# Two chunks of a weight product in float32r from split parts, and one activation load issued a chunk sooner

## The chip, the cores and the metric

The kernel runs on one core of one Trainium2 chip. The metric is the device time of one execution in microseconds (us). One execution was recorded by the hardware profiler; its rows carry the line of the kernel (L573 is line 573), the engine and the tiles. PE is the matrix engine, PEld its weight loads, DVE the vector engine, ACT the scalar engine, POOL the general-purpose engine, SP the engine that issues most DMAs. A row with SPq is an issue by SP's sequencer.

## The reference

Attention against a small state in both directions, then a bilinear layer with no nonlinearity but a product, the weights in float64 on their way into the chip:

```python
def _attn_ref(x, state):                  # x: 8 x 8 x 512 x 64, state: 8 x 8 x 32 x 64
    ...
    xread = np.matmul(a, state)           # a = softmax(x state^T / 8)
    ...
    sread = np.matmul(a2, x)              # a2 = softmax(state x^T / 8)
    return np.concatenate([xread, sread], axis=2).astype(np.float32)

def _moe_ref(x, w1, w2, w3, w_out):       # x: 4352 x 512 here; w1, w2: 512 x 1024
    a = x @ w1
    b = x @ w2
    h = a * b @ w3                        # w3: 1024 x 1024
    return (h @ w_out).astype(np.float32) # w_out: 1024 x 512
```

Since nothing stands between w3 and w_out, the kernel multiplies these two once, at its start (w34 = w3 w_out, 1024 x 512), and uses the result for all tokens.

## The kernel before

**Stages.** The program has a prologue of about 70 us and then eight batches. A batch multiplies the attention weights by state-times-w1 and state-times-w2 (stage 1, L321), takes the product of the two results, and multiplies it by w34 (stage 2, L335, and for batches 1 to 7 the quarters of L435 to L453). A row block of read states follows at the end. The prologue makes w34, the first attention scores and the first weights of stage 1. The change lies in the prologue alone.

**The loads and their conversion.** The weights arrive as float64 bits, 1 MB for a tile of 128 x 1024 words. `to_f32` (L103 to L137) loads such a tile into one of three `raw` buffers (L115, issued by SP) and makes float32 of it: on ACT the high words (L119, Prelu), then the low words into `ulps` (L127); after its `yield` on DVE a shift (L131) and the adding of the two (L135). The raw buffer is free again when L127 has read it. Loads 0 and 1 are done in two parts, the others in one.

**The order of the prologue.** PE, SP, ACT and DVE run in the order of the program there (`manual_schedule`, L65 and L609). `w34_k[k]`, k = 0 to 7, holds in one tile w_out's k-th 128 rows (512 columns) and four blocks of w3 for the same k (512 columns). L612 to L615 convert such a tile per step and, two steps later, multiply it: `w34_first` (L570 to L576) has four float32 products of 128 x 128 by 128 x 512 per k, each adding to one of four PSUM sums. In steps 8 and 9 two blocks of another tensor, w3t, are loaded and converted (`convert_w3`, L578). Behind the loop come, in this order:

- `load_x(0)` (L616): st and x_d of batch 0, 64 KB and 1 MB, issued by SP;
- the scores of batch 0 on PE (L148, from `scores`, L180);
- `finish(0)`, `finish(1)` and a split of the sums 2 and 3 together (L620 to L622): a cast on ACT (L98) and a subtraction on DVE (L99), which give the high and low part of w34 in float32r;
- `w34(4)` (L623): eight products by the block of w3t that step 8 converted, into the PSUM bank that `finish(0)` has read;
- the conversion of w1 and w2 and of the last two w3t blocks, the softmax of batch 0 (L187 to L233), `w34(5)`, `w34(6)`, and so on.

`split` (L95) is used all over: `hi` is a float32r copy of its source by ACT, `lo` the difference by DVE. Stage 1 has three products for each full one: hi by lo, hi by hi, lo by hi. `sw_pair` (L272) takes a pair of float32r tiles of 128 x 2 x 512 from a rotation of four.

Of the kernel before, what the change touches and what calls it, by code (L numbers as in the profile page):

```python
# [29 lines left out]
P = 128  # L30
NF = 512
NW = 1024
AHEAD = 2
LAST = 5
PARTS = {0: (640, 1024), 1: (512, 1024)}
WARM = 15
PLAIN = 1

@with_exitstack
def attn_bilinear_kernel(  # L40
# [10 lines left out]
    nc = tc.nc  # L51
# [5 lines left out]
    FT, DO = w34_k.shape[0], out.shape[2]  # L57
# [31 lines left out]
    def bank():  # L89
        return ps_o.tile([P, NF], F32, name="ps_o")  # L90

    def two_banks():
        return ps_2.tile([P, 2, NF], F32, name="ps_2")

    def split(hi, lo, src):  # L95

        return (
            nc.scalar.copy(out=hi, in_=src),  # L98
            nc.vector.tensor_tensor(out=lo, in0=src, in1=hi.bitcast(F32), op=ALU.subtract),  # L99
        )  # L100


    def to_f32(pool, src, out, ends=(NW,), loads=(), wout=None):  # L103

        raw = pool.tile([P, NW], mybir.dt.int64, name="raw", bufs=3)
        ulps = pool.tile([P, NW], I32, name="ulps", bufs=2)
        parts = [slice(*ends) for ends in zip((0, *ends), ends)]
        for start, stop in zip((0, *loads), (*loads, NW)):
            nc.sync.dma_start(out=raw[:, start:stop], in_=src[:, start:stop])  # L115
        for part in parts:
            words = raw[:, part].bitcast(I32).rearrange("p (n k) -> p k n", k=2)
            high, low = words[:, 1], words[:, 0]
            nc.scalar.activation(  # L119
                out=out[:, part], in_=high.bitcast(F32), func=AF.Prelu, scale=2.0**-112, alpha=-(2.0**32)  # L120
            )
            if len(parts) > 1:
                nc.vector.tensor_scalar(
                    out=ulps[:, part], in0=low.bitcast(U32), scalar1=2.0**-29, scalar2=None, op0=ALU.mult
                )
            else:
                nc.scalar.activation(out=ulps[:, part], in_=low.bitcast(U32), func=AF.Copy, scale=2.0**-29)  # L127
        yield
        for part in parts:
            bits = out[:, part].bitcast(I32)  # L130
            nc.vector.tensor_scalar(out=bits, in0=bits, scalar1=3, scalar2=None, op0=ALU.logical_shift_left)  # L131
            for dest, start, stop in ((wout, 0, DO), (out, DO, NW)) if wout is not None else ((out, 0, NW),):
                piece = slice(max(start, part.start), min(stop, part.stop))
                if piece.start < piece.stop:
                    nc.vector.tensor_tensor(  # L135
                        out=dest[:, piece].bitcast(I32), in0=out[:, piece].bitcast(I32), in1=ulps[:, piece], op=ALU.add
                    )  # L137
# [14 lines left out]
    def load_x(b):  # L152
        sts[b] = att.tile([P, NP, NS], F32, name="st")
        nc.sync.dma_start(out=sts[b], in_=st[b])
        x_tiles[b] = att.tile([P, NP, S], F32, name="x_d", bufs=1)
        nc.sync.dma_start(out=x_tiles[b], in_=x_d[b])
# [8 lines left out]
    def work_tile():  # L165
        return att.tile([P, KT, S], F32, name="work")
# [9 lines left out]
    def attention_steps(b):  # L176
# [3 lines left out]
        def scores():  # L180
# [15 lines left out]

            first, second = (maxima, turn) if b > PLAIN else (turn, maxima)
            with tc.issue_after(first().ins):
# [4 lines left out]
            for kt in range(KT):  # L203
# [3 lines left out]
                )  # L207
            if b > PLAIN:
                yield
# [27 lines left out]
            with tc.issue_after(last[1].ins):  # L237
                nc.vector.transpose(out=flat(blocks), in_=flat(e2))
            a2["t"] = work_tile() if b < PLAIN else att.tile([P, KT, S], F32, name="e2", bufs=1)
            tiles = lambda t: t.rearrange("p k (t m) -> p (k t) m", m=P)  # L240
# [31 lines left out]
    def sw_pair():  # L272
        return [main.tile([P, KT, NF], F32R, name=f"sw_{part}", bufs=2 * HALF) for part in ("hi", "lo")]
# [244 lines left out]
    def quarter_batch(b):  # L518
        q = {"raw": []}
        softmax = iter(())  # L520
        for ft in range(FT):
# [19 lines left out]
            elif ft == 4:  # L541
                next(softmax, None)
            if b == PLAIN and ft == 1:
                combine_weights(QF - 1)
# [4 lines left out]
    def run(steps):  # L549
        for step in steps:  # L550
            for _ in step() or ():
                pass


    with tc.tile_pool(name="pro", bufs=2) as pro:

        places = [w_sb[:, n // 2, n % 2].rearrange("p j f -> p (j f)") for n in range(2 * QT)]
        w_out = [places[(FT + k) // 2][:, k % 2 * DO:(k % 2 + 1) * DO] for k in range(FT)]

        chunks = [places[k % (FT // 2)] for k in range(FT)]  # L560
        w3s, w34_ps = {}, {}

        def finish(i):
            split(wo["hi"][:, i], wo["lo"][:, i], w34_ps[i][:, :DO])

        def convert_first(k):
            ends = PARTS.get(k, (NW,))
            return to_f32(pro, w34_k[k], chunks[k], ends, (), wout=w_out[k])

        def w34_first(k):  # L570

            for i in range(FT // 2):
                nc.tensor.matmul(  # L573
                    w34_ps[i][:, :DO], chunks[k][:, DO + i * P:DO + (i + 1) * P], w_out[k],
                    start=(k == 0), stop=(k == FT - 1),
                )  # L576

        def convert_w3(i):  # L578
            w3s[i] = pro.tile([P, NW], F32, name="w3", bufs=2)
            return to_f32(pro, w3t[i - FT // 2], w3s[i])  # L580

        def w34(i, ks=range(FT)):
            if ks[0] == 0:
                w34_ps[i] = bank()
            for k in ks:
                nc.tensor.matmul(  # L586
                    w34_ps[i][:, :DO], w3s[i][:, k * P:(k + 1) * P], w_out[k], start=(k == 0), stop=(k == FT - 1)
                )

        def convert_half(n):  # L590

            return to_f32(pro, w12[n], places[n])

        def sets(quarter):
            for i in range(2):
                sw_quarter(0, quarter, i)


        gs, acc, early = [], [], range(2)

        def early_stage2(quarter):
            if quarter == 0:
                acc.extend(bank() for _ in early)
            for ft in range(2 * quarter, 2 * quarter + 2):
                for tt in early:
                    project(acc[tt], gs, tt, ft)

        order = ctx.enter_context(ExitStack())
        order.enter_context(tc.manual_schedule(engines={mybir.EngineType.Activation, mybir.EngineType.DVE}))  # L609
        pair = two_banks()  # L610
        w34_ps.update(enumerate([bank(), bank(), pair[:, 0], pair[:, 1]]))
        for k in range(FT + AHEAD):  # L612
            run([partial(convert_first, k) if k < FT else partial(convert_w3, k - FT // 2)])
            if k >= AHEAD:
                w34_first(k - AHEAD)  # L615
        load_x(0)  # L616
        scores, reads[0], _ = attention_steps(0)
        softmax = scores()
        next(softmax)
        finish(0)  # L620
        finish(1)
        split(wo["hi"][:, 2:4], wo["lo"][:, 2:4], pair[:, :, :DO])  # L622
        w34(4)  # L623

        w1_0, w2_0, w1_1, w2_1 = map(convert_half, range(4))
        go = lambda steps: next(steps, None)
        w3_6 = convert_w3(6)
        go(w1_0), go(softmax), go(w1_0)
        finish(4)
        go(w2_0), go(w3_6), go(softmax), go(w3_6)  # L630
        w34(5)
        go(softmax)
        go(w2_0)
        finish(5)
        w3_7 = convert_w3(7)
        go(w3_7), go(w3_7), go(w1_1), go(w1_1), go(w2_1), go(w2_1)
        load_tokens(0)
        w34(6)
        sets(0)
        finish(6)  # L640
        w34(7, range(LAST))
        sets(1)
        w34(7, range(LAST, FT))
        finish(7)
        order.close()
        for quarter in range(QT):
            stage1(0, 2 * quarter, gs)
            if quarter == 1:
                run(sw_steps(0)[2:])
            if quarter:  # L650
                early_stage2(quarter - 1)
            if quarter == 1:
                side = side_steps()
            elif quarter == 2:
                run(side.pop(0))
            stage1(0, 2 * quarter + 1, gs)
            if quarter == 0:
                run([partial(convert_half, n) for n in range(4, 2 * QT)])
                load_x(1)
                with tc.issue_after(last_split[1].ins):  # L660
                    go(softmax)
        run(side.pop(0))
        early_stage2(QT - 1)
# [42 lines left out]

    for b in range(PLAIN, B):
        quarter_batch(b)
# [46 lines left out]
```

## Time and profile before

| | |
|---|---|
| median of 3 runs | 490.66 us (490.65 to 491.01) |
| the profiled execution | 490.49 us |
| its span, first to last instruction | 488.7 us |
| mean granted PE clock | 0.998 |
| HBM read, written | 38.27 MB, 8.91 MB |

The span is shorter than the time of its execution by what lies before the first and behind the last instruction. Busy times are unions of an engine's instructions. A matmul of float32 gives two records, one of float32r gives one, and the end of each is modelled, so that rates are read from start to start. In the view of 40 equal slices PE is busy in every slice, and DMA is busiest in the first six, which are the prologue.

### The profile page before, as it was taken

The page shows a single profiled execution, that of the slowest core. Times are in us where ns is not written, and L with a number is a line of the kernel's source. Part 1 is how long each engine was busy: PE and PEld are TensorE (multiplying, and loading weights), DVE is VectorE, ACT ScalarE, POOL GpSimd, SP SyncE. Part 2 cuts the span into 40 slices and gives each one's busy share as a digit, 9 for nine tenths or more (in the row PEclk, how much of TensorE's full clock was granted, in tenths as well). Part 3 has the DMA queues.
Part 4 walks back from the last instruction along what each step waited for, and adds up shares of the span by engine and source line. Part 5 has one row for each costly group of instructions (what it writes and reads, how often), then busy time and mean ns, then how long its engine had stood idle before and what let it go on. Part 6 is the DMA issues. An engine that isn't in the chain of part 4 may idle for free.

```text
span 488.7 us, 8603 instructions
## 1 busy us (share of the span) xinstructions
PE 482.1 (99%) x3390; PEld 368.9 (75%) x3390; DVE 391.0 (80%) x576; ACT 235.5 (48%) x364; POOL 0.2 (0%) x4
## 2 busy tenths in 40 slices
PE   8999999999999999999999999999999999999996
PEld 6444467767787878887888788877977797899885
DVE  5669897699899679958995899599859985678870
ACT  4767784454357144704570556055515541353640
POOL 0000000000000000000000000000000000000000
PEclk9999999999999999999999999999999999999999
DMA  8996981153114404130413041304230223001101
GB/s 343 359 368 242 369 307 27 18 206 73 37 20 165 118 15 166 48 98 4 180 37 96 4 181 41 90 5 180 44 86 6 89 44 87 5 2 43 45 1 44
DMA packets 56361, 52.49 MB, mean 107 GB/s; under 512 B 42752, under 2 KB 50944, under 8 KB 51712
## 3 DMA queue, kind: packets, MB, share of 16 engines
q1 hardware_dynamic: 47488, 43.27, 27.0%
q10 hardware_dynamic: 8832, 8.65, 5.2%
q8 instruction: 27, 0.44, 0.4%
q14 instruction: 14, 0.11, 0.1%
HBM read 38.27 MB, written 8.91 MB: 97 GB/s over the span
## 4 chain that ended last, share of the span: by engine, by line
PE 77%; DVE 7%; SPq 6%; ACT 5%; DMA 3%; issue 1%; ACTq 0%; DVEq 0%
PE ps L321 29%; PE ps_o L435 11%; PE ps L447 8%; PE ps L148 6%; SPq L172 6%; PE ps_o L440 5%; PE ps L452 4%; PE ps L693 3%; PE ps_o L573 3%; PE ps L573 3%; PE ps_o L335 2%; DMA raw<-in_w_dram 2%; PE ps L695 2%; ACT ulps L127 2%; PE ps_o L253 1%
## 5 line engine op out<-in xcount | busy, mean ns | idle before, releaser
L321 PE MATMUL ps<-at_lo,sw_hi 128*128 128x512 f32 x256 | 101.3, 396 | 0.2 <-ACT e L205 0.2
L321 PE MATMUL ps<-at_hi,sw_hi 128*128 128x512 f32 x256 | 99.7, 390 | 0.0
L321 PE MATMUL ps<-at_hi,sw_lo 128*128 128x512 f32 x256 | 99.7, 389 | 0.0
L525 ACT COPY tmp<-ps 128x512 f32<-128x512 f32 x56 | 32.8, 585 | 121.6 <-PE ps L321 121.1
L321 PEld LDWEIGHTS ps<-at_lo,sw_hi 128*128 128x128 f32 x256 | 48.1, 188 | 16.9 <-DVE g_lo L99 4.2
L321 PEld LDWEIGHTS ps<-at_hi,sw_lo 128*128 128x128 f32 x256 | 48.1, 188 | 10.3
L321 PEld LDWEIGHTS ps<-at_hi,sw_hi 128*128 128x128 f32 x256 | 48.1, 188 | 9.4 <-issue 0.2
L463 DVE TENSOR_TENSOR tmp<-tmp,ps 128x512 f32<-128x512 f32 x42 | 28.8, 687 | 17.8 <-PE ps L452 16.9
L404 DVE TENSOR_TENSOR g_x<-tmp,ps 128x512 f32<-128x512 f32 x28 | 19.0, 678 | 28.1 <-ACT tmp L525 28.1
L99 DVE TENSOR_TENSOR sw_lo<-ps,sw_hi 128x1024 fp32r<-128x1024 f32 (+1 forms) x34 | 38.2, 1145 | 1.5 <-ACT sw_hi L98 1.5
L98 ACT CAST g_hi<-raw 128x512 fp32r<-128x512 f32 x42 | 24.6, 619 | 28.1 <-DVE raw L404 20.7
L435 PEld LDWEIGHTS ps_o<-t,g_hi 128*128 128x128 f32 x224 | 27.7, 191 | 5.5 <-issue 5.0
L148 PE MATMUL ps<-w_sb,st 64*32 64x512 f32 (+1 forms) x544 | 31.4, 570 | 0.0
L98 ACT CAST sw_hi<-ps 128x1024 fp32r<-128x1024 f32 (+1 forms) x34 | 31.1, 966 | 0.6 <-PE ps L148 0.5
L98 ACT CAST g_hi<-g_x 128x512 fp32r<-128x512 f32 x42 | 25.5, 626 | 11.4 <-DVE g_x L404 6.0
L435 PE MATMUL ps_o<-t,g_hi 128*128 128x256 f32 x224 | 29.8, 286 | 0.3 <-ACT tmp L483 0.3
L99 DVE TENSOR_TENSOR g_lo<-raw,g_hi 128x512 fp32r<-128x512 f32 x42 | 27.9, 678 | 1.7 <-PE ps_o L440 1.6
L435 PE MATMUL ps_o<-wo,g_hi 128*128 128x256 f32 x224 | 29.1, 283 | 0.0
L435 PEld LDWEIGHTS ps_o<-wo,g_hi 128*128 128x128 f32 x224 | 28.3, 192 | 0.5
L586 PE MATMUL ps_o<-w_sb,w 128*128 128x512 f32 x64 | 28.5, 599 | 0.0
L99 DVE TENSOR_TENSOR g_lo<-g_x,g_hi 128x512 fp32r<-128x512 f32 x42 | 27.1, 679 | 1.8 <-PE ps_o L440 1.8
L447 PE MATMUL ps<-t,g_hi 128*128 128x512 f32 x112 | 28.0, 392 | 0.0
(103 smaller groups left out, 784.6 us busy)
## 6 DMA issues: line engine op xcount, KB each, us to landing
raw<-in_w_k_dram SPq DMA_DIRECT2D x8, 1024.0 KB, 6.7
x_d<-in_x_d_dram SPq DMA_DIRECT2D x8, 1024.0 KB, 6.8
raw<-in_w_dram SPq DMA_DIRECT2D x8, 1024.0 KB, 6.8
x_s<-in_x_s_dram SPq DMA_DIRECT2D x8, 1024.0 KB, 5.0
out_dram<-tmp ACTq DMA_DIRECT2D x56, 128.0 KB, 1.8
raw<-in_w3t_dram SPq DMA_DIRECT2D x4, 1024.0 KB, 7.4
e<-work SPq DMA_DIRECT2D x112, 32.0 KB, 2.0
sread<-turned SPq DMA_DIRECT2D x128, 4.0 KB, 1.7
```

The costliest lines, as they stand in the source:

```text
L98: nc.scalar.copy(out=hi, in_=src),
L99: nc.vector.tensor_tensor(out=lo, in0=src, in1=hi.bitcast(F32), op=ALU.subtract),
L148: nc.tensor.matmul(ps[j * NS:(j + 1) * NS, q], sts[b][rows, j], moving(rows, j), start=True, stop=True)
L172: nc.sync.dma_start(out=dest(slice(c * NS, (c + 1) * NS), j), in_=src(slice(j * NS, (j + 1) * NS), c))
L321: nc.tensor.matmul(ps[:, i], w[:, kt, c:c + P], a[:, kt], start=(k == 0), stop=(k == 3 * KT - 1))
L435: nc.tensor.matmul(ps[:, tt * HO:(tt + 1) * HO], g, w(part, k), start=(fresh and k == 0 and tt == 0 and part == "lo"), stop=False, skip_gr ...
L440: nc.tensor.matmul(ps[:, tt * HO:(tt + 1) * HO], g, w("hi", k), start=False, stop=(k == QF - 1), skip_group_check=True)
L447: nc.tensor.matmul(ps[:, tt].rearrange("p (n d) -> p n d", n=2), g, w(k), start=(k == 0), stop=False, skip_group_check=True,)
L463: sum2 = lambda out, x, y: nc.vector.tensor_tensor(out=out, in0=x, in1=y, op=ALU.add)
L525: copied = nc.scalar.copy(out=a_sb, in_=ps[:, 0])
L573: nc.tensor.matmul(w34_ps[i][:, :DO], chunks[k][:, DO + i * P:DO + (i + 1) * P], w_out[k], start=(k == 0), stop=(k == FT - 1),)
L586: nc.tensor.matmul(w34_ps[i][:, :DO], w3s[i][:, k * P:(k + 1) * P], w_out[k], start=(k == 0), stop=(k == FT - 1))
```

## The change

1. Chunks k = 4 and k = 6 (`SPLIT`) are no longer multiplied in float32. Their w_out half and their w3 half are each split into a high and a low part in float32r (`split_of`, two casts on ACT and two subtractions on DVE), and `w34_first` has three float32r products for each of the four sums, twelve in all, instead of four float32 ones.
2. The splitting of chunk k is issued inside the conversion of chunk k + 1: on ACT and DVE behind L119 of that chunk and ahead of its L127 (`between`).
3. `load_x(0)` is issued ahead of step 9 of the loop instead of behind the loop: SP issues st and x_d of batch 0 ahead of the second w3t block, not behind it.

```diff
+SPLIT = (4, 6)
...
-    def to_f32(pool, src, out, ends=(NW,), loads=(), wout=None):
+    def to_f32(pool, src, out, ends=(NW,), loads=(), wout=None, between=None):
...
             nc.scalar.activation(
                 out=out[:, part], in_=high.bitcast(F32), func=AF.Prelu, scale=2.0**-112, alpha=-(2.0**32)
             )
+            if between:
+                between()
             if len(parts) > 1:
...
-            return to_f32(pro, w34_k[k], chunks[k], ends, (), wout=w_out[k])
+            return to_f32(pro, w34_k[k], chunks[k], ends, (), wout=w_out[k], between=split_of(k - 1))
+
+        halves = {}
+
+        def split_of(k):
+            if k not in SPLIT:
+                return None
+
+            def both():
+                halves[k] = sw_pair()
+                for n, src in enumerate((w_out[k], chunks[k][:, DO:])):
+                    split(*(t[:, n] for t in halves[k]), src)
+
+            return both
 
         def w34_first(k):
 
+            if k in SPLIT:
+                hi, lo = halves[k]
+                for i in range(FT // 2):
+                    cols = slice(i * P, (i + 1) * P)
+                    for a, b in ((hi, hi), (hi, lo), (lo, hi)):
+                        nc.tensor.matmul(w34_ps[i][:, :DO], a[:, 1, cols], b[:, 0], start=False, stop=False)
+                return
...
         for k in range(FT + AHEAD):
+            if k == FT + AHEAD - 1:
+                load_x(0)
             run([partial(convert_first, k) if k < FT else partial(convert_w3, k - FT // 2)])
             if k >= AHEAD:
                 w34_first(k - AHEAD)
-        load_x(0)
         scores, reads[0], _ = attention_steps(0)
```

## The prediction

> **What bounds the kernel now.** I read the page first, then the prologue (0 to 70 us) in the timelines of PE, ACT, DVE and SP, because the change touches nothing behind it.
>
> ```profile
> span 488.7 us, 8603 instructions
> PE 482.1 (99%) x3390; PEld 368.9 (75%) x3390; DVE 391.0 (80%) x576; ACT 235.5 (48%) x364; POOL 0.2 (0%) x4
> ```
>
> PE is busy for 99% of the span: what delays PE anywhere moves the end by as much, and what shortens PE work pays only if the next operand is there. So I ask which operand PE waits for in the prologue. The timeline of PE:
>
> ```profile
> 1.05 5.82 PE L77 MATMUL ps_o<-work 128*128 128x128 f32 x30 [1.05 <-DVE work L74]
> ...
> 21.97 1.88 PE L573 MATMUL ps_o<-w_sb 128*128 128x512 f32 x4
> 23.69 1.88 PE L573 MATMUL ps<-w_sb 128*128 128x512 f32 x4
> 25.41 1.88 PE L573 MATMUL ps_o<-w_sb 128*128 128x512 f32 x4
> ...
> 35.80 1.09 PE L148 MATMUL ps<-x_d,st 64*32 64x512 f32 x16
> 36.82 21.18 PE L586 MATMUL ps_o<-w_sb,w 128*128 128x512 f32 x48
> ```
>
> One chunk is 8 records from 21.97 to 25.41: 3.43 us for 4 products, 0.86 each. I call the chunks M0 to M7; M4 starts at 21.97, M5 at 25.41, so M6 at 28.84, M7 at 32.27, and the scores of batch 0 (L148) at 35.80. Then come three blocks of L586, w34(4), (5), (6), of 8 products. Their 24 products need 24 x 0.86 = 20.6, the row lasts 21.18: some waiting is hidden in it. The waits of 5 to 60 us name it, and DVE's timeline says when it ends:
>
> ```profile
> PEld ps_o L586 <- DVE w L135: 1.3, 2, 0.9
> ```
> ```profile
> 18.34 1.29 DVE L135 CUSTOM_DVE_ANT_0 w_sb<-w_sb,ulps 128x1024 uint16<-128x1024 uint16 x2 [0.34 <-ACT ulps L127]
> ...
> 33.03 0.69 DVE L131 TENSOR_SCALAR w<-w 128x1024 int32<-128x1024 int32 x1 [0.56 <-ACT w L119]
> 34.09 1.23 DVE L135 CUSTOM_DVE_ANT_0 w<-w,ulps 128x2048 uint16<-128x2048 uint16 x1 [0.36 <-ACT ulps L127]
> 35.23 1.28 DVE L99 TENSOR_TENSOR wo<-ps_o,wo 128x512 fp32r<-128x512 f32 x2
> 36.95 1.23 DVE L99 TENSOR_TENSOR wo<-ps,wo 128x1024 fp32r<-128x1024 f32 x1 [0.44 <-ACT wo L98]
> 38.09 1.24 DVE L191 STREAM_TRANSPOSE work<-ps 128x1024 f32<-128x1024 f32 x1
> ...
> 49.59 1.23 DVE L135 CUSTOM_DVE_ANT_0 w<-w,ulps 128x2048 uint16<-128x2048 uint16 x1
> ```
>
> w34(6) needs the w3 block whose conversion ends at 49.59 + 1.23 = 50.82; by its own work PE would be there at 36.82 + 16 x 0.86 = 50.6. **DVE is 0.2 us the later of the two**, and it is busy nearly throughout (the view by windows; DVE is the third sum):
>
> ```profile
> 35.00:51.00 16.00, 15.95 (x52) 6.36 (x51) 15.08 (x21) 10.37 (x14) 0.00 (x0) 1.00 0.73 283
> ```
>
> What stands at the head of that DVE run decides: the conversion of load 9 (L131 33.03, L135 34.09; I count the prologue's loads 0 to 7 as w_out|w3 chunks, 8 and 9 as w3t blocks), then the splits of the w_out-times-w3 sums (L99, `finish`), then the softmax. ACT's timeline shows what load 9 waits for. An L119 row that waited for DMA starts as its load lands:
>
> ```profile
> 5.58 1.27 ACT L119 ACTIVATE w_sb<-raw 128x640 f32<-128x640 f32 x2 [3.58 <-DMA raw<-in_w_k_dram]
> ...
> 19.93 1.14 ACT L119 ACTIVATE w_sb<-raw 128x1024 f32<-128x1024 f32 x1 [1.63 <-DMA raw<-in_w_k_dram]
> 20.97 1.15 ACT L127 ACTIVATE ulps<-raw 128x1024 int32<-128x1024 uint32 x1
> 22.39 1.16 ACT L119 ACTIVATE w_sb<-raw 128x1024 f32<-128x1024 f32 x1 [0.27 <-DMA raw<-in_w_k_dram]
> 23.45 1.15 ACT L127 ACTIVATE ulps<-raw 128x1024 int32<-128x1024 uint32 x1
> 24.82 1.16 ACT L119 ACTIVATE w_sb<-raw 128x1024 f32<-128x1024 f32 x1 [0.22 <-DMA raw<-in_w_k_dram]
> ...
> 29.02 1.14 ACT L119 ACTIVATE w<-raw 128x1024 f32<-128x1024 f32 x1 [1.98 <-DMA raw<-in_w3t_dram]
> ...
> 31.85 1.15 ACT L119 ACTIVATE w<-raw 128x1024 f32<-128x1024 f32 x1 [0.64 <-DMA raw<-in_w3t_dram]
> ...
> 33.96 1.05 ACT L98 CAST wo<-ps_o 128x512 fp32r<-128x512 f32 x2
> 35.91 1.01 ACT L98 CAST wo<-ps 128x1024 fp32r<-128x1024 f32 x1 [0.90 <-PE ps L573]
> 36.95 1.17 ACT L119 ACTIVATE w_sb<-raw 128x1024 f32<-128x1024 f32 x1
> ```
>
> Loads 5 to 9 land at 19.9, 22.4, 24.8, 29.0 and 31.85. SP's issues, and x's time to landing (the view of tile x_d):
>
> ```profile
> 0.73 1.35 SPq L115 DMA_DIRECT2D raw<-in_w_k_dram  x3
> ...
> 22.15 0.33 SPq L115 DMA_DIRECT2D raw<-in_w3t_dram  x1
> ...
> 24.63 0.33 SPq L115 DMA_DIRECT2D raw<-in_w3t_dram  x1
> 25.00 0.43 SPq L154 DMA_DIRECT2D st<-in_st_dram  x1
> 25.48 0.46 SPq L156 DMA_DIRECT2D x_d<-in_x_d_dram  x1
> ```
> ```profile
> DMA to landing us min/median/max: 9.0/9.0/9.0
> ```
>
> Load 8 is issued (22.15) when ACT has read load 5 out of the raw buffer (20.97 + 1.15), load 9 (24.63) when it has read load 6 (23.45 + 1.15). x lands at 25.48 + 9.0 = 34.5, 1.3 us ahead of its use at 35.80.
>
> **The change, part by part.** *Products.* The float32r row nearest is stage 1, start to start:
>
> ```profile
> 80.40 0.39 PE L321 MATMUL ps<-at_hi,sw_hi 128*128 128x512 f32 x1
> 80.63 0.39 PE L321 MATMUL ps<-at_hi,sw_lo 128*128 128x512 f32 x1
> ```
>
> 0.23 each, 12 per chunk: 2.73 instead of 3.43, so 0.70 less per chunk, **1.4 us at most** (0.29%).
>
> *Splits.* Each adds two casts on ACT and two subtractions on DVE. Rows of this shape, from the page:
>
> ```profile
> L98 ACT CAST g_hi<-raw 128x512 fp32r<-128x512 f32 x42 | 24.6, 619 | 28.1 <-DVE raw L404 20.7
> L99 DVE TENSOR_TENSOR g_lo<-raw,g_hi 128x512 fp32r<-128x512 f32 x42 | 27.9, 678 | 1.7 <-PE ps_o L440 1.6
> ```
>
> On ACT the next row starts 0.1 before the end of the one ahead (19.93 + 1.14 against 20.97), so two casts cost 1.03. They stand between L119 and L127 of the next chunk. Chunk 4: its words are ready at 18.34 + 1.29 = 19.6, but ACT casts only after load 5's L119, from 20.97; casts end at 21.6 and 22.1, subtractions at 22.3 and 22.9. M4, due at 21.97, has its third product wait until 22.9; ten more follow: end 22.9 + 10 x 0.23 = 25.2 instead of 25.41. **M4 gains 0.2, not 0.7.** Load 5's L127 moves from 20.97 to 22.0 and ends at 23.15; its add on DVE ends at 24.85, still ahead of M5 (25.2 to 28.6). For chunk 6 the same reckoning puts the second cast behind the add of chunk 6 (26.8), its subtraction at 28.2: ahead of M6 at 28.6 by 0.4, which is the cover. M6 takes 2.73, M7 3.43: the scores can start at 34.8 instead of 35.7, **0.9 earlier**. If the cover were gone, the price is the lateness itself.
>
> *What the splits delay.* L127 of loads 5 and 6 releases the buffers of loads 8 and 9: load 8 is issued at 23.2 instead of 22.15, load 9 at 25.3 instead of 24.63. L127 of load 7 goes from about 25.9 to 27.3; the load behind it (w1) is deep in the queue, so nothing.
>
> *The moved load.* st and x are issued behind load 8, at 23.6 and 24.1, and load 9 behind them. x is then early (needed at 34.8). Load 9 is now the third megabyte instead of the second. Its landing is the unknown of the sum:
> - Load 8: from issue to landing 4.85 when nothing is under way (0.73 to 5.58), 6.87 when issued 2.67 before the landing ahead (22.15 to 29.02, landing ahead 24.82). Now it is issued 1.6 before that landing. Between the two rows: about 6.0, landing at 29.2. Bounds 28.05 and 30.1.
> - x and load 9 behind it: 2.45 each in a full queue (19.93, 22.39, 24.82), 2.83 in the thinner one (29.02 to 31.85); st, 1/16 of x, 0.15. I take 2.45, since both are issued over 4 us ahead of the landing before them.
> - Load 9 lands at 29.2 + 0.15 + 4.9 = **34.25** instead of 31.85; bounds 33.1 and 35.9.
>
> A separate remark from the Trainium skill, "DMA: Bandwidth & Descriptors", section on the anatomy of one DMA: a fixed 2.0 us plus bytes over 436 GB/s. By it load 8 alone would take 4.4, and the sum below would come to about +0.3 us; the row of 4.85 is near it, the row of 6.87 is not.
>
> *What waits for load 9.* On ACT and DVE the order is written out: conversion of load 9, then the splits of sums 0 and 1, then of the pair 2/3. Queued behind load 9's L119 on ACT are all three casts; who waits is DVE, and PE, since w34(4) writes the bank that the split of sum 0 reads. By the rows, the split of sum 0 starts on DVE 35.23 - 31.85 = 3.38 after the landing and lasts 0.68: 38.3. **PE stands idle from 35.8 to 38.35** and w34(4) starts 1.5 late. The pair's subtraction starts at 34.25 + 3.38 + 1.2 = 38.85 instead of 36.95: the DVE run is **1.9 late**. Before, that subtraction waited for PE's M7 (0.90 on ACT, 0.44 on DVE); this goes, and what is late next is DVE's own queue. In general the shift is the landing of load 9 less 32.35.
>
> *Sum.* w34(6) starts when its block is converted, 50.82 + 1.9; PE would be there 0.6 earlier. Loads further on (w1, w2, w3 blocks 6, 7) are issued when ACT releases buffers and move by no more than 1.9. Behind it PE has no idle to take it up. The profiled execution took 490.49 (span 488.7 and 1.8 around it), so 492.4 against its own; the median before, 490.66, is 0.17 above it: **492.6 us**. That the products cost what I say hardly matters: anything PE gains before 38.35 is lost in the wait.
>
> **The rivals.**
> - *Not slower: the transfers close up.* The 4.2 us between the landings of loads 7 and 8 is 1.75 more than a full queue needs. If load 8, x and load 9 run gapless behind load 7, load 9 lands at 24.82 + 7.35 + 0.15 = 32.3, a shift of 0; up to a landing of 33.3 the shift stays under 1.0 (0.2%). For: x fills the queue 1.4 earlier. Against: load 8 is issued a microsecond later than now and already came late. About 491.1.
> - *Faster.* If load 9 landed under 31.5, ahead of or beside x, M7's 0.9 would reach the end: 489.8. Against: it needs three megabytes in 6.7 us, and no stretch of landings is that quick.
> - *PE falls to a slow clock in its idle 2.5 us.* The first row above has 30 records of 128 columns in 5.82; at the later rate (0.43 for 512) they need 3.2, so after idling PE started slowly here. 3.4 us at half rate would cost 1.7, less the 0.6 that w34(6) waits anyway: 493.7. In the Trainium skill, "TensorE: Matmul & The Clock Gate", section on the clock gate, the clock drops after a wholly idle window of about 3.4 us. By that rule an idle of 2.5 us leaves it alone; no run here shows it yet.
> - *The change doesn't do what it says:* float32r products no cheaper here. Then M4 and M6 gain nothing, the scores start at about 36.5, still ahead of 38.35: 492.6 again.
>
> **How the numbers follow.** The forecast has 0.70, closing transfers 0.15, faster 0.07, slow clock 0.05, no cheaper products 0.03. About 0.2% is what a measurement here tells from no change. Slower: 0.70 + 0.05 + 0.03 = 0.78; same 0.15; faster 0.07. The bounds of the landing give +0.7 to +3.5, so 491.4 to 494.2; taking in most of the closing case and cutting the last of the late end, the range is 490.8 to 494.0.
>
> **What would show it.** In the profile after: L119 of load 9 starting near 34 (not 32); the three products of M4 with a wait for ACT or DVE near 22; L586 idle before its first product for 2 to 3 us, released by DVE wo L99; scores near 34.8; w34(6) near 52.7; SP with x ahead of the second w3t load. Wrong would be a load 9 that lands before 33.3, or a later stage that gives back the shift.

## The result and the profile after

The changed kernel takes 492.31 us (median of 22 runs, 490.54 to 494.20), the kernel before in the same runs 490.82 (490.34 to 491.95). The ratio is 1.0031, with a 95% interval of 1.0022 to 1.0039: slower by 1.5 us. The forecast was 492.6. The profiled execution of the changed kernel took 493.12, so it lies 0.8 above its median, and the landing of load 9 below is probably later than a typical one.

The page of the changed kernel:

```profile
span 491.3 us, 8623 instructions
PE 481.3 (98%) x3398; PEld 370.9 (75%) x3398; DVE 393.0 (80%) x580; ACT 237.2 (48%) x368; POOL 0.2 (0%) x4
```

PE works 0.8 us less than before (482.1) and DVE 2.0 more: that is the change as written. The span is 2.6 longer all the same, so PE stands idle for 3.4 more. Its timeline (start, duration, instruction; in brackets the idle time ahead and what ended it) says where. The lines have moved: L609 is the block product that was L586, L596 the float32 chunk product, L593 the float32r one.

```profile
34.54 1.09 PE L151 MATMUL ps<-x_d,st 64*32 64x512 f32 x16
39.15 14.00 PE L609 MATMUL ps_o<-w_sb,w 128*128 128x512 f32 x32 [3.52 <-DVE wo L100]
53.50 7.13 PE L609 MATMUL ps_o<-w_sb,w 128*128 128x512 f32 x16 [0.35 <-DVE w L138]
```

In the kernel before, the first record of w34(6) is:

```profile
50.87 0.70 PE L586 MATMUL ps_o<-w_sb,w 128*128 128x512 f32 x1
```

The scores start at 34.54 instead of 35.80: PE did gain 1.26 us in the chunks. Then it waits 3.52 us for DVE's split of sum 0, and w34(4) starts at 39.15 instead of 36.82. w34(6) starts at 53.50 instead of 50.87, **2.63 later**, and the span ends 2.6 later: nothing behind it gave anything back. SP, ACT and DVE of the changed kernel, in this order, one view each:

```profile
22.47 0.33 SPq L116 DMA_DIRECT2D raw<-in_w3t_dram  x1
22.85 0.42 SPq L157 DMA_DIRECT2D st<-in_st_dram  x1
23.32 0.42 SPq L159 DMA_DIRECT2D x_d<-in_x_d_dram  x1
24.56 0.33 SPq L116 DMA_DIRECT2D raw<-in_w3t_dram  x1
```
```profile
19.21 1.15 ACT L120 ACTIVATE w_sb<-raw 128x1024 f32<-128x1024 f32 x1 [0.74 <-DMA raw<-in_w_k_dram]
20.27 1.12 ACT L99 CAST sw_hi<-w_sb 128x512 fp32r<-128x512 f32 x2
...
29.97 1.14 ACT L120 ACTIVATE w<-raw 128x1024 f32<-128x1024 f32 x1 [1.16 <-DMA raw<-in_w3t_dram]
...
35.08 1.14 ACT L120 ACTIVATE w<-raw 128x1024 f32<-128x1024 f32 x1 [2.92 <-DMA raw<-in_w3t_dram]
...
37.13 1.06 ACT L99 CAST wo<-ps_o 128x512 fp32r<-128x512 f32 x2
38.08 1.03 ACT L99 CAST wo<-ps 128x1024 fp32r<-128x1024 f32 x1
```
```profile
37.27 1.22 DVE L138 CUSTOM_DVE_ANT_0 w<-w,ulps 128x2048 uint16<-128x2048 uint16 x1 [0.33 <-ACT ulps L130]
38.41 1.28 DVE L100 TENSOR_TENSOR wo<-ps_o,wo 128x512 fp32r<-128x512 f32 x2
39.61 1.21 DVE L100 TENSOR_TENSOR wo<-ps,wo 128x1024 fp32r<-128x1024 f32 x1
...
52.22 1.22 DVE L138 CUSTOM_DVE_ANT_0 w<-w,ulps 128x2048 uint16<-128x2048 uint16 x1
```

Load 9 is issued at 24.56, practically when it was before (24.63), but behind x. It lands at 35.1 instead of 31.85. ACT is idle for 2.92 us ahead of it although PE is through with the sums by then (the scores behind them start at 34.54), because their casts stand behind the conversion of load 9 in ACT's order. The pair's subtraction starts at 39.61 instead of 36.95, 2.66 late, and this is what w34(6) shows: the conversion of its block on DVE ends at 53.44, and w34(6) starts at 53.50.

### The profile page after: what moved, and what is told of

The parts are those of the page before. It is cut to its first block, busy times and chain, and to the rows that moved or that the text cites. A ratio compares the mean times of both kernels' runs of the same rounds, so it can differ in the third digit from the quotient of the medians.

```text
span 491.3 us, 8623 instructions
## 1 busy us (share of the span) xinstructions
PE 481.3 (98%) x3398; PEld 370.9 (75%) x3398; DVE 393.0 (80%) x580; ACT 237.2 (48%) x368; POOL 0.2 (0%) x4
## 4 chain that ended last, share of the span: by engine, by line
PE 71%; DMA 8%; DVE 7%; ACT 6%; SPq 6%; issue 2%; ACTq 0%; DVEq 0%
PE ps L324 29%; PE ps_o L438 11%; PE ps L450 8%; SPq L175 6%; PE ps L151 6%; PE ps_o L443 5%; PE ps L455 4%; DMA raw<-in_w_k_dram 3%; PE ps L717 3%; PE ps_o L338 2%; DMA raw<-in_w3t_dram 2%; ACT ulps L130 2%; DMA raw<-in_w_dram 2%; PE ps L719 2%; ACT w_sb L120 1%
## 5 line engine op out<-in xcount | busy, mean ns | idle before, releaser
L609 PE MATMUL ps_o<-w_sb,w 128*128 128x512 f32 x64 | 28.5, 599 | 3.9 <-DVE wo L100 3.5
L151 PE MATMUL ps<-w_sb,st 64*32 64x512 f32 (+1 forms) x544 | 31.4, 570 | 0.0
```

What stands on the lines that cost most here:

```text
L151: nc.tensor.matmul(ps[j * NS:(j + 1) * NS, q], sts[b][rows, j], moving(rows, j), start=True, stop=True)
L609: nc.tensor.matmul(w34_ps[i][:, :DO], w3s[i][:, k * P:(k + 1) * P], w_out[k], start=(k == 0), stop=(k == FT - 1))
```

## The experiments

Two theories were put against each other. **A**: load 9 lands late because x goes ahead of it, and the casts and subtractions of the sums, in the written order behind its conversion, carry that on to PE. **B**: the splits' own work on ACT and DVE is the loss. Later a second question came up, why the time of the changed kernel scatters. Each kernel is compared with the kernel before in the same runs, whose medians were 490.8 to 490.9; the ratio is not the quotient of the two medians.

| kernel | median us (lowest to highest) | ratio to before, 95% interval |
|---|---|---|
| the change | 492.31 (490.54 to 494.20) | 1.0031 (1.0022 to 1.0039) |
| splits only | 490.14 (489.88 to 490.64) | 0.9982 (0.9973 to 0.9990) |
| x moved only | 493.28 (490.73 to 495.13) | 1.0042 (1.0024 to 1.0060) |
| the change, load 9 early | 490.32 (489.62 to 491.27) | 0.9987 (0.9978 to 0.9995) |
| the change, sums before load 9 | 492.44 (491.46 to 493.99) | 1.0036 (1.0022 to 1.0050) |
| load 8 early, x behind load 9, splits | 490.25 (489.35 to 490.54) | 0.9983 (0.9974 to 0.9992) |
| load 8 early, x behind load 9, no splits | 490.71 (490.51 to 491.64) | 0.9999 (0.9990 to 1.0008) |
| load 8 early, x behind load 9, splits of 4, 5 and 6 | 490.79 (489.49 to 491.82) | 0.9995 (0.9984 to 1.0005) |
| load 8 early, x behind load 9, 4 and 6 split at once | **489.29 (489.21 to 489.56)** | **0.9969 (0.9959 to 0.9979)** |
| load 8 early, x behind load 9, 4, 6 and 7 split at once | 491.07 (490.40 to 491.42) | 1.0002 (0.9993 to 1.0011) |

**Splits only** (e1_split_only): x goes back behind the loop.

```diff
-            if k == FT + AHEAD - 1:
-                load_x(0)
...
+        load_x(0)
         scores, reads[0], _ = attention_steps(0)
```

> Chunks 4 and 6 in float32r as in the change, x of batch 0 loaded behind the second w3t block as before. Theory A (load 9, the second w3t block, lands late because x goes ahead of it; the end shifts by its landing less 32.35 us): load 9 is the second megabyte behind load 7 again and lands at 32 to 33, x at about 35, PE's idle before L609 under 1 us, time within 0.7 us of the kernel before (490.2 to 491.5). Theory B (the casts and subtractions of the splits delay ACT and DVE, and the order of the loads matters little): about as slow as the whole change, 492 to 492.6.

It is faster than the kernel before, by 0.8 us in the medians (before 490.92 in these runs). Its ACT, then PE:

```profile
31.36 1.15 ACT L120 ACTIVATE w<-raw 128x1024 f32<-128x1024 f32 x1 [0.55 <-DMA raw<-in_w3t_dram]
...
34.50 1.01 ACT L99 CAST wo<-ps 128x1024 fp32r<-128x1024 f32 x1
```
```profile
35.17 1.09 PE L151 MATMUL ps<-x_d,st 64*32 64x512 f32 x16 [0.71 <-DMA x_d<-in_x_d_dram]
36.20 20.89 PE L609 MATMUL ps_o<-w_sb,w 128*128 128x512 f32 x48
```

Load 9 lands at 31.4 (32 to 33 expected) and the pair's cast starts at 34.50 instead of 35.91. x is late now: PE waits 0.71 for it. That is what the moved load was to remove, and the wait costs far less than removing it did. Theory B falls as the cause of the loss: all of the splits' work is in here, and nothing is lost. The time came out just below the expected range.

**x moved only** (e2_move_only): the kernel before with the three lines of the loop.

```diff
+            if k == FT + AHEAD - 1:
+                load_x(0)
             run([partial(convert_first, k) if k < FT else partial(convert_w3, k - FT // 2)])
...
-        load_x(0)
         scores, reads[0], _ = attention_steps(0)
```

> x of batch 0 loaded ahead of the second w3t block as in the change, all chunks in float32 as before. Theory A: load 9 is the third megabyte, issued about 1 us sooner than with the splits; it lands at about 34.3, idle before w34(4) about 2 us, time 492 to 493. Theory B: no splits, no loss: 490.5 to 491.0.

ACT, then PE:

```profile
34.38 1.14 ACT L119 ACTIVATE w<-raw 128x1024 f32<-128x1024 f32 x1 [2.90 <-DMA raw<-in_w3t_dram]
```
```profile
35.91 1.09 PE L148 MATMUL ps<-x_d,st 64*32 64x512 f32 x16
38.51 14.00 PE L586 MATMUL ps_o<-w_sb,w 128*128 128x512 f32 x32 [1.50 <-DVE wo L99]
52.87 7.13 PE L586 MATMUL ps_o<-w_sb,w 128*128 128x512 f32 x16 [0.37 <-DVE w L135]
```

The whole loss is there without a split. The landing, 34.4, gives 50.87 + 34.38 - 32.35 = 52.90 for w34(6); it is 52.87. PE's idle before w34(4) is 1.50 (about 2 expected). The median is 0.3 above the expected range, and the runs spread over 4.4 us.

**The change, load 9 early** (e3_load9_early): the second w3t block gets a raw tile of its own, the one that later takes the tokens of batch 0, and is issued behind load 7. x stays where the change puts it.

```diff
+        def load_spare(i):
+            spare[i] = att.tile([P, NW], mybir.dt.int64, name="x_s", bufs=1)
+            nc.sync.dma_start(out=spare[i], in_=w3t[i - FT // 2])
...
-            return to_f32(pro, w3t[i - FT // 2], w3s[i])
+            return to_f32(pro, w3t[i - FT // 2], w3s[i], raw=spare.pop(i, None))
...
         for k in range(FT + AHEAD):
+            if k == FT:
+                load_spare(5)
             if k == FT + AHEAD - 1:
                 load_x(0)
```

> The whole change, but the second w3t block (load 9) goes into the tile that later takes the tokens of batch 0, so that it is issued right behind load 7, at about 19, ahead of load 8 and of x. Splits and the place of x are those of the change. Theory A: load 9 lands before load 8 (about 27 to 28), load 8 at about 30; the conversions of both are done by 34.5, the pair's subtraction on DVE starts near 36.1 instead of 39.6, and the time is 0.5 to 1.2 us under the kernel before: 489.6 to 490.3. Theory B: the splits still cost their time, 492 or more.

DVE:

```profile
34.09 1.23 DVE L139 CUSTOM_DVE_ANT_0 w<-w,ulps 128x2048 uint16<-128x2048 uint16 x1 [0.27 <-ACT ulps L131]
35.23 1.28 DVE L100 TENSOR_TENSOR wo<-ps_o,wo 128x512 fp32r<-128x512 f32 x2
36.43 1.22 DVE L100 TENSOR_TENSOR wo<-ps,wo 128x1024 fp32r<-128x1024 f32 x1
```

The pair's subtraction starts at 36.43, 0.5 earlier than in the kernel before and 3.2 earlier than in the change, with the same splits and x in the same place. That is theory A's link taken out by itself. The gain is at the small end of what was expected, since here load 8 is the one that DVE waits for: its conversion and that of load 9 follow each other without a break.

**The change, sums before load 9** (e4_finish_first): the splits of the sums 0 to 3 are written ahead of the conversion of load 9.

```diff
         for k in range(FT + AHEAD):
...
-            run([partial(convert_first, k) if k < FT else partial(convert_w3, k - FT // 2)])
+            if k < FT + AHEAD - 1:
+                run([partial(convert_first, k) if k < FT else partial(convert_w3, k - FT // 2)])
...
         split(wo["hi"][:, 2:4], wo["lo"][:, 2:4], pair[:, :, :DO])
+        run([partial(convert_w3, FT + AHEAD - 1 - FT // 2)])
```

> The whole change, but the splits of the sums 0 to 3 stand ahead of the conversion of load 9 on ACT and DVE. The landing of load 9 is late as in the change (34 to 35). Theory A, with the written order on ACT and DVE as the link: PE's idle before w34(4) goes (w34(4) starts near 35.7), DVE's run gets the 1.9 us of load 9's conversion in place of the wait, w34(6) starts near 51.7, and the time is about 0.9 us over the kernel before: 491.2 to 492.0. If the link were another (the load or x itself), nothing changes: 492.3.

PE:

```profile
34.46 1.09 PE L151 MATMUL ps<-x_d,st 64*32 64x512 f32 x16
35.48 14.00 PE L609 MATMUL ps_o<-w_sb,w 128*128 128x512 f32 x32
51.64 7.13 PE L609 MATMUL ps_o<-w_sb,w 128*128 128x512 f32 x16 [2.16 <-DVE w L138]
```

Load 9 was late here too: it was issued at 24.28 and took 9.6 us, so it landed at 33.9. With w34(4) 4.1 behind that landing, as in the change, w34(4) would start at 38.0. That wait is gone: w34(4) starts at 35.48, 1.02 behind the scores, as long as the scores take. w34(6) starts at 51.64 (51.7 expected), because DVE now has load 9's conversion ahead of the softmax. So the written order is the link. But this execution (491.46) was the fastest of six; the median, 492.44, was a miss. The same kernel was profiled once more:

> The same kernel as e4_finish_first, for a second trace: its profiled execution (491.46) was the fastest of six, and their median (492.44) was over the forecast. Theory A has the conversion of load 9 still on DVE ahead of the softmax: a landing after 35.5 would move the end by as much as it is later. So a slower execution must show load 9 landing after 35.5, with w34(6) later than 51.64 by the same amount; if it lands before 35.5 and the time is over 492, something else is late.

This execution took 492.62. PE, then ACT; and behind it ACT of the first execution:

```profile
35.60 1.09 PE L151 MATMUL ps<-x_d,st 64*32 64x512 f32 x16
36.62 14.00 PE L609 MATMUL ps_o<-w_sb,w 128*128 128x512 f32 x32
52.79 7.13 PE L609 MATMUL ps_o<-w_sb,w 128*128 128x512 f32 x16 [2.17 <-DVE w L138]
```
```profile
20.45 1.13 ACT L120 ACTIVATE w_sb<-raw 128x1024 f32<-128x1024 f32 x1 [2.61 <-DMA raw<-in_w_k_dram]
```
```profile
18.94 1.14 ACT L120 ACTIVATE w_sb<-raw 128x1024 f32<-128x1024 f32 x1 [0.70 <-DMA raw<-in_w_k_dram]
```

Something else was late, and not load 9, which ACT could take only at 36.61 though it had landed by 33.6 (issued at 25.7, 7.8 to landing): the scores themselves, by 1.14, and w34(6) by the same 1.15. The row that differs is load 5. It landed 1.5 later here, and the casts of chunk 4 stand behind it (they start at 21.47 instead of 19.98). So in the change a PE step, M4, hangs on a transfer that it has nothing to do with. The two slowest of the six, 493.69 and 493.99, are more than another microsecond later; neither was traced.

**Load 8 early, x behind load 9** (e5_load8_early): the spare tile takes load 8 (`load_spare(4)`), x goes back behind the loop. Nothing that a sum or the scores wait for should then be late.

> Splits of chunks 4 and 6 as in the change; the first w3t block (load 8) goes into the tile that later takes the tokens of batch 0 and is issued right behind load 7; x of batch 0 behind load 9, as before the change. Theory A: loads 8, 9 and x land near 27, 30 and 32.5; neither the conversion of load 9 nor x is late, so M7's end sets DVE's run: the pair's subtraction starts near 35.6 (36.95 before), and the time is 0.9 to 1.4 us under the kernel before: 489.4 to 490.0. If the splits cost their own time on ACT and DVE, 490.6 or more.

The profiled execution (489.35, the fastest of 11) is as expected; the median, 490.25, is not. PE and DVE:

```profile
34.39 1.09 PE L152 MATMUL ps<-x_d,st 64*32 64x512 f32 x16
```
```profile
35.55 1.23 DVE L100 TENSOR_TENSOR wo<-ps,wo 128x1024 fp32r<-128x1024 f32 x1 [1.45 <-ACT wo L99]
```

Here load 5 landed earliest of all traces:

```profile
18.00 1.16 ACT L121 ACTIVATE w_sb<-raw 128x1024 f32<-128x1024 f32 x1 [0.25 <-DMA raw<-in_w_k_dram]
```

**The same without splits** (`SPLIT = ()`, e6_early_no_split) tells the early load from the products:

> The load order and buffers of e5_load8_early, but no chunk is split: all eight in float32. Theory A: PE's M7 ends at 35.7 as before and DVE's run starts at most 0.44 us sooner than before (its wait for ACT there): 490.3 to 491.0. The difference to e5_load8_early is what the float32r products are worth once nothing is late: 0.7 to 1.2 us. If the early load itself were the gain, it would be as fast as e5_load8_early.

490.71 is the time of the kernel before (490.81 in these runs). Its scores start at 35.99 and the pair's subtraction at 37.15, no sooner than before (35.80 and 36.95). So the early load is worth nothing by itself; the gain is the products'. Splits only, which has no early load, was as fast (490.14). The difference to the kernel with splits, 0.5 in the medians, was below the 0.7 expected.

**Chunk 5 split too** (`SPLIT = (4, 5, 6)`, e7_three_splits):

> As e5_load8_early with chunk 5 split too. PE saves another 0.7 us at most; ACT gets 1.0 and DVE 1.3 us more between loads 6 and 8, where ACT has 2.1 us of conversion per 2.45 us of landing. If there is room: 488.8 to 489.4. If ACT and DVE are full by then: no faster than e5_load8_early, M6 or M7 waiting for DVE.

490.79, no gain. In its profile, PE:

```profile
25.59 0.50 PE L594 MATMUL ps_o<-sw_hi 128*128 128x512 f32 x1
...
29.01 0.50 PE L594 MATMUL ps_o<-sw_hi 128*128 128x512 f32 x1
...
32.15 1.88 PE L597 MATMUL ps_o<-w_sb 128*128 128x512 f32 x4
```

M5 starts at 25.59, M6 at 29.01, M7 at 32.15: 3.42 and 3.14 from chunk to chunk although each has only 2.73 of products. Each split stands behind the next load's L121, and ACT is full there: L121 starts at 19.89, 23.00, 26.49 and 29.91, so a chunk with its split takes ACT 3.1 to 3.5 us, longer than PE's 2.73. The splits come late, and the scores start at 35.68, hardly sooner than without any split (35.80 in the kernel before, 35.99 in this one without splits).

**Split at once** (e8_split_at_once): chunk k is split behind its own conversion, not behind L119 of chunk k + 1. Loads as in "load 8 early".

```diff
-            return to_f32(pro, w34_k[k], chunks[k], ends, (), wout=w_out[k], between=split_of(k - 1))
+            return to_f32(pro, w34_k[k], chunks[k], ends, (), wout=w_out[k])
...
             run([partial(convert_first, k) if k < FT else partial(convert_w3, k - FT // 2)])
+            if k in SPLIT:
+                split_of(k)()
```

> As e5_load8_early, but chunk k is split right behind its own conversion, not behind the landing of load k + 1. Theory: in the change M4 waits for a split that waits for load 5, and load 5 lands anywhere from 18 to 20.4 in the traces so far (M4 22.65 and the scores 35.60 where it landed at 20.36, the scores 34.39 where it landed at 17.92). With the split at once M4 starts at its time (21.6 to 22.0) in every execution, so the median falls to what the fastest executions of e5_load8_early had, 489.3 to 489.8, with less spread than its 1.2 us. If the spread has another cause, 490.2 as before.

489.29, and eight runs within 0.35 us. **This beats both kernels**, the one before by 0.31% (0.21% to 0.41%). ACT, then PE, then DVE:

```profile
18.86 1.22 ACT L99 CAST sw_hi<-w_sb 128x512 fp32r<-128x512 f32 x2 [0.76 <-DVE w_sb L139]
19.99 1.16 ACT L121 ACTIVATE w_sb<-raw 128x1024 f32<-128x1024 f32 x1
```
```profile
34.52 1.09 PE L152 MATMUL ps<-x_d,st 64*32 64x512 f32 x16
35.54 21.18 PE L616 MATMUL ps_o<-w_sb,w 128*128 128x512 f32 x48
```
```profile
35.67 1.23 DVE L100 TENSOR_TENSOR wo<-ps,wo 128x1024 fp32r<-128x1024 f32 x1 [0.71 <-ACT wo L99]
```

The casts end at 20.1, ahead of M4, and no longer hang on load 5; they stand ahead of its L121 now and hold that up where load 5 lands early, which M5 has the cover for. Load 5 landed early in this trace (issued at 12.74, 6.1 to landing: 18.8); the next experiment shows the same order with a late one.

**Chunk 7 split too**, in that kernel (`SPLIT = (4, 6, 7)`, e9_three_at_once):

> As e8_split_at_once with chunk 7 split too (its cast and subtraction fall into a gap of ACT and DVE ahead of the sums). M7 takes 2.7 instead of 3.4 us: another 0.4 to 0.7 us, 488.7 to 489.3. If DVE or ACT is late there (the conversion of load 9 moves back by 1.0 to 1.3 us), no faster than e8_split_at_once.

PE, then DVE:

```profile
21.68 0.80 PE L594 MATMUL ps_o<-sw_hi 128*128 128x512 f32 x1
...
37.08 14.00 PE L618 MATMUL ps_o<-w_sb,w 128*128 128x512 f32 x32 [1.75 <-DVE wo L100]
```
```profile
35.19 1.22 DVE L139 CUSTOM_DVE_ANT_0 w<-w,ulps 128x2048 uint16<-128x2048 uint16 x1 [0.29 <-ACT ulps L131]
36.34 1.28 DVE L100 TENSOR_TENSOR wo<-ps_o,wo 128x512 fp32r<-128x512 f32 x2
```

491.07, 1.8 slower than with two splits: the third split pushes the conversion of load 9 on DVE to an end at 36.4 instead of 33.8 (1.0 to 1.3 us later were expected, it is 2.6), the sums behind it, and PE waits 1.75 for them. It is theory A's queue again, filled by work and not by a landing. The trace also settles what split at once does: load 5 landed at 20.2 (issued at 12.86, 7.3 to landing), as late as in the slower execution of the kernel with the sums before load 9, and M4 starts at 21.68 all the same.

**The change once more** (after_again), for a second landing:

> The changed kernel once more, for a second trace: the start of w34(6) should lie at 50.87 plus the landing of load 9 less 32.35, within 0.2 us, whatever that landing is; PE should stand idle before w34(4) until 4.1 us behind that landing.

ACT, then PE (491.94 us):

```profile
20.07 1.13 ACT L120 ACTIVATE w_sb<-raw 128x1024 f32<-128x1024 f32 x1 [1.98 <-DMA raw<-in_w_k_dram]
...
33.38 1.14 ACT L120 ACTIVATE w<-raw 128x1024 f32<-128x1024 f32 x1 [2.48 <-DMA raw<-in_w3t_dram]
```
```profile
35.23 1.09 PE L151 MATMUL ps<-x_d,st 64*32 64x512 f32 x16
37.49 14.00 PE L609 MATMUL ps_o<-w_sb,w 128*128 128x512 f32 x32 [1.18 <-DVE wo L100]
51.86 7.13 PE L609 MATMUL ps_o<-w_sb,w 128*128 128x512 f32 x16 [0.37 <-DVE w L138]
```

33.38 gives 50.87 + 1.03 = 51.90; it is 51.86. PE's wait ends at 37.49, 4.1 behind the landing.

## Why the prediction was right, point by point

- **The queue behind load 9.** Shown, by three landings with x ahead (35.08, 34.38, 33.38: w34(6) at 53.50, 52.87, 51.86; the rule gives 53.60, 52.90, 51.90), by taking the lateness away (load 9 early), by undoing each part of the change alone, and by turning the order round.
- **The landing of load 9.** Forecast 34.25, bounds 33.1 and 35.9. The two traces of the change have 33.4 and 35.1. The median, 1.5 above that of the kernel before, fits a landing near 33.8 by the rule; that was not measured over the runs. Load 8 did not land as the forecast interpolated: it took 7.5 and 5.0 us from its issue in the two traces, not 6.0, with bounds of 4.85 and 6.87. Behind it load 9 landed 5.1 later both times (5.05 forecast). So in these two traces the difference is load 8's. The mechanism was foreseen, but that the median came within 0.3 us of the forecast is in part luck.
- **PE's idle before w34(4).** Forecast 2.5; 1.18 and 3.52, by the landing.
- **The products.** Forecast 0.23 each; in the second trace of the change the 12 of M6 follow each other every 0.23, which makes 2.7. Right, and lost in the wait, as said.
- **M4 and the splits.** Forecast: M4 gains 0.2 since its casts stand behind load 5, and the scores start at 34.8. This term was right in kind and wrong in size: M4 gained 0.7 in the first trace of the change and nothing in the second, where M5 starts at 25.53 (25.2 forecast, 25.41 before). There PE waits for both casts and starts at 22.29, where the prediction let only the third product wait. The prediction took load 5's landing from one trace, 19.93, as if it were fixed. Landings of load 5 (by ACT's row) and starts of the scores in five traces with this order: 18.00 and 34.39, 18.94 and 34.46, 19.21 and 34.54, 20.07 and 35.23, 20.45 and 35.60. Up to 19.2 the splits are in time and M4 gains nearly all its 0.7; beyond, each microsecond is passed on. In the change this decides nothing while load 9 is late; in the kernels without that wait it is what scatters.
- **No later give-back.** The 2.63 at w34(6) are 2.6 at the end of the span in the one trace; in the second, 0.99 at w34(6) became 1.4; where the other 0.4 came from stays open.
- **The rivals.** The transfers did not close up: from load 8 to load 9 it took 5.1 us in the first trace of the change, two full megabytes and a little. The faster side would have needed load 9 ahead of x; where it was (splits only), the time was 0.18% under the kernel before. In the two traces the slow clock did not come: behind 3.52 us of idle the 32 records of L609 take 14.00, as in the kernel with load 9 early, where nothing was idle ahead of them. In other executions it probably did, as the next point says.
- **The clock.** Once PE is under way, the granted clock of all 13 traces falls to 0.50 only behind PE's last product, between 2.0 us (x moved only) and 5.3 us (split at once) after it. What this takes off the mean over the span is at most 0.002. So the 74 runs of the kernel before beside the experiments have 0.998 to 1.000, and no run with load 9 ahead of x has less than 0.998. But four of the 22 runs of the change have 0.997 or 0.995 (493.14, 493.59, 493.91 and 494.20 us), and so have the five slowest of the twelve with x moved only (0.997, 494.27 to 495.13) and the slowest of the six with the sums before load 9 (0.997, 493.99). A mean of 0.997 is 1.5 us of lost clock, about 3 us at half clock. These ten most likely had a slow stretch ahead of their end, behind a long idle of PE; none of them was traced, so where it lay and what it cost is not shown. The forecast gave this rival 0.05. Without the four runs the median of the change is 492.1, so this is not what made the change slower. In the Trainium skill, "TensorE: Matmul & The Clock Gate", section on the clock gate, the gate closes after a whole idle window of about 3.4 us in a free-running count. The traces differ: 2.0 us behind the last product is sooner than a wholly idle window allows, while the idle of 3.52 left the clock alone. So the prediction's reading that an idle of 2.5 us is safe is not borne out.

Partly open: why x moved alone is slower in the median (493.28) than the whole change (492.31). Without the runs at 0.997 or less the medians are 492.59 and 492.10, so about half of the difference goes with the clock. Its one trace follows the same rule as the change; that its load 9 lands later on the average was not shown.

## What to carry to other kernels

A load moved ahead in a full queue delayed the load behind it by its own transfer (load 9 landed 5.1 us behind load 8 instead of 2.8); before moving one, look which of the loads behind it the in-order engines meet first, and what else stands behind that instruction in their written order. A wait of 0.7 us on the busiest engine can be cheaper than its removal, as splits only shows. Put a step that only needs data already there in front of, not behind, the wait for the next transfer, or a steady step takes over the scatter of the transfer.

## What the runs showed of the hardware

The landing of one and the same load scatters far more than engine work does (here 2.45 us, where the ACT instruction that reads it takes 1.13 to 1.16). Load 5 is issued between 12.6 and 12.9 in all 13 traces, and the rows above have it landing anywhere from 18.0 to 20.45. The kernel before had 2.0 us of cover for it (the conversion ends at 23.44, M5 starts at 25.41), and its times span 1.6 us; the changed kernel's span 3.7, and the one that splits at once, 0.35. So a wide spread of the runs can be a sign that a transfer stands bare on the path; what makes the 1.6 us of the kernel before was not looked into.
